# An H3 block with a gated feed-forward: the order of the first loads, the banks of the first transposes, and the first two feed-forward units by halves

## The chip, the cores and the metric

The kernel runs on one core of a Trainium2 chip. The core has TensorE (PE: matrix multiplications and transposes into PSUM), VectorE (DVE), ScalarE (ACT), GpSimd (POOL) and the sync engine (SP, which here issues most DMAs). PSUM has eight banks of 128 partitions x 512 float32; sixteen DMA engines move data between device memory and SBUF. The metric is device time in microseconds of one execution, as a median over runs; lower is better. Before the change it is 215.22 us, the median of 8 runs (214.69 to 217.48).

## The reference

All data is bfloat16, 2048 rows of 512 columns. With `x` = `A_q`, cut to what is computed:

```
xn = layernorm(x)                                   # per row of 512
kv = (4-tap causal shift of k with shift_k) * v     # per column
y  = causal convolution of kv with ssm_k (length 2048, one filter per column) + kv * ssm_D
s  = xn * y
g  = silu( (gelu(xn @ w_gate) * (xn @ w_up)) @ w_down )   # 512 -> 1792 -> 512
out = x + s * g
```

The reference does the convolution with an FFT of length 4096.

## The kernel before

**The convolution.** The kernel does the Fourier transform as matrix multiplications in two stages. Row 16p + t of a tensor lies on partition p of tile t, so there are 16 tiles of 128 x 512. In stage 1 (`stage1`, line 900) each tile t is multiplied by a table F1[t] of cosines and sines (two matmuls of 512 columns); ScalarE copies the result out of PSUM, and a DMA writes it to device memory (ZH for the filter h, ZK for kv), from where stage 2 reads it back in another layout. Stage 2 (`fwd`) multiplies by the table MT. For the filter the result goes to ZS and is read back as HS; for kv it is multiplied with HS on VectorE (line 1015, tile HB), transformed back with MT (`inv`, line 1019), copied by ScalarE (BO), written to ZI and read back as BI; eight last multiplications with G1 (the transposed F1) give y. The filter comes as 512 channels x 2048 taps, so it is first transposed on TensorE: four chunks of 128 channels (tile Hn, loads h0 to h3), each as two halves of 8 transposes (`h_transpose`, line 812, transposes on line 823), copied out as HTr by VectorE or ScalarE. D is added to tap 0 by one VectorE instruction (`h_fold`, line 836). Stage 1 of the filter needs all of HTr and the fold.

**The feed-forward.** The 2048 rows are treated as four quarters q of four tiles. `ln(q)` (line 759) makes mean and variance of each tile on VectorE (bn_stats, line 762; bn_aggr, line 763; variance plus epsilon, line 770), takes the power -0.5 on POOL (line 771) and normalises on VectorE (line 774, tile XN). `xn_transpose(q)` transposes: for q = 0 on TensorE (line 796) in two halves of two tiles, each into a bank and copied to xnT (line 801); for the others by a DMA transpose (line 786). `unit(q, m)` (line 1043) computes 128 of the 1792 hidden columns for a quarter: four matmuls of 512 columns for the gate, four for the up part, Gelu on ScalarE (GE, line 1058), a product on VectorE (HT, line 1061). `down(q)` (line 1064) multiplies HT by w_down, 14 matmuls for each tile, followed by tanh or silu and the products with xn and y.

**Tables.** F1 and MT are made on the chip: iotas on POOL, integer work on VectorE (lines 651 to 669 and 865 to 889), Sin on ScalarE (line 675, 891). Gelu needs another table of ScalarE, so its first use waits until every Sin of F1 is done (`sin_tasks`).

**Order.** The order of instructions on each engine is written by a planner, `Sched.run` (line 313). Each piece of work is a task with an assumed duration, the buffers it needs and a priority (lower goes first). The planner takes the engine that can start earliest, looks at the tasks that could start within SLACK ns of that, and takes the one of lowest priority number; a TensorE task marked `heavy="DVE"` or `"ACT"` has DEFER added when the queue of work for that engine, counted from tasks of priority up to URGENT, is over QUEUE. HEDGE is the delay that it assumes after a DMA for TensorE. The order is then fixed; on the chip each engine works through its list and waits for semaphores. Loads are issued ahead of everything else, in the order of the `load` calls from line 745 on: x of the first quarter as four tiles of 128 KB, h0, h1, the first weight chunk (gate and up), h2, h3, D, the shift taps, and then ORDER (line 25). Most are issued by SP, a few by ACT, whose queue is another ring of the same sixteen DMA engines.

**PSUM.** Pool psF hands out single banks (at most 4 at a time) for units, down tiles and the xn transposes; psC hands out pairs (at most 3) of the same eight banks for the stages and, before the change, for the h transposes. A bank becomes free when the engine that reads it is done.

**Warm-up.** N_WARM matmuls on zeros run before the first data is there.

Of the kernel before, what the change touches and what calls it, by code (L numbers as in the profile page):

```python
# [17 lines left out]
KD = DM // 128  # L18
# [5 lines left out]
N_WARM = 18  # L24
# [235 lines left out]
class Sched:  # L260


    SLACK = 269.06
    SEM = 90.0
    DMA_LAT = 2500.0
    HEDGE = 2000.5
# [4 lines left out]
    QUEUE = {"ACT": 600, "DVE": 4110.2}  # L271
    URGENT = 3.36
    DEFER = 4.48
# [119 lines left out]
def build_kernel(nc, A_q, A_k, A_v, A_shift_k, A_ssm_k, A_ssm_D, B_w_gate, B_w_up, B_w_down, out):  # L393
    with ExitStack() as es0:
# [156 lines left out]
        pC = Pool_("psC", 4, size=2, limit=NC_PAIRS, backing=pF)  # L551
        pGE = Pool_("GE", 3)
# [80 lines left out]
        t_warm = S.add([("PE", 1700.0 + N_WARM * 216.0)], warm_up, r=[bwarm], w=[warm], prio=-9)  # L633
# [70 lines left out]
        FC = [(0, 4), (4, 4), (8, 4), (12, 2)]  # L704
# [7 lines left out]
        def load_x(q):  # L712
            if q:
                load(f"x{q}", X[:, 4 * q:4 * q + 4, :], x_dr[:, 4 * q:4 * q + 4, :], R_X[4 * q:4 * q + 4], bX[q], 524288)
            else:
                for t in range(4):
                    load(f"x{q}_{t}", X[:, t, :], x_dr[:, t, :], R_X[t:t + 1], [bX[0][t]], 131072, ("SP", "ACT")[t % 2])
# [27 lines left out]
        load_x(0)  # L745
        load_h(0, "SP")
        load_h(1, "ACT")
# [11 lines left out]
        def ln(q):  # L759
            pr = (-1, 2, 3.27, 6)[q]  # L760
            for t in range(4 * q, 4 * q + 4):
                op([("DVE", 670.0)], lambda e, h, t=t: h.bn_stats(stats[:, t, :], X[:, t, :]), r=[bX[q][t % 4]], w=[bst[t]], rr=[R_X[t]], ww=[R_st[t]], prio=pr)  # L762
                op([("DVE", 140.0)], lambda e, h, t=t: h.bn_aggr(mv[:, t, 0:2], stats[:, t, :]), r=[bst[t]], w=[bmv[q][t % 4 // 2]], rr=[R_st[t]], ww=[R_mv[t]], prio=pr)
            for h in range(1 if q else 2):
                n = 4 if q else 2
                ts = slice(4 * q + 2 * h, 4 * q + 2 * h + n)
# [3 lines left out]
                op([("DVE", 180.0)], lambda e, hd, ts=ts: hd.tensor_scalar(mv[:, ts, 2:3], mv[:, ts, 1:2], LN_EPS, None, ALU.add), r=bm, w=[be], rr=rm, ww=rm, prio=pr)  # L770
# [10 lines left out]
        def xn_transpose(q):  # L781
            af = gu_tasks[q - 2] if q >= 2 else (mt_last + skb if q else [])
            if q:
# [4 lines left out]
                return  # L788
            for hf in range(2):
                p = B(f"psxn{q}_{hf}", pF)  # L790

                def tr(e, hf=hf, p=p):
                    for j in (2 * hf, 2 * hf + 1):
                        for kd in range(KD):
                            o = bank16(p)[:, 512 * (j % 2) + 128 * kd:512 * (j % 2) + 128 * (kd + 1)]
                            trk.op("PE", lambda h, o=o, kd=kd, j=j: h.transpose(o, XN[:, 4 * q + j, 128 * kd:128 * (kd + 1)], ident[:]),
                                   r=[R_XN[4 * q + j], R_id], w=R_bank(p), accum=True)
                S.add([("PE", 8 * 66.0)], tr, r=[bid] + bXN[4 * q + 2 * hf:4 * q + 2 * hf + 2], w=[p], prio=0, lat=200.0)

                def ev(e, h, hf=hf, p=p):  # L800
                    return copy(e, h, xnT[:, q % 2, 2 * hf:2 * hf + 2, :, :].rearrange("p j k c -> p (j k c)"), bank16(p))
                xnT_tasks.append(op([("DVE", dve(1024, 2)), ("ACT", act(1024))], ev, r=[p], w=[bxnT[q][hf]],
                   rr=lambda p=p: R_bank(p), ww=R_xnT[q % 2][2 * hf:2 * hf + 2], prio=-1, after=af))
# [8 lines left out]
        def h_transpose(k):  # L812
            p = B(f"psh{k}", pC)
            pp = [B(f"psh{k}_{h}") for h in range(2)]

            def tr(hf):
                def f(e):
                    s = psl(p)
                    for j in range(8):
                        t = 8 * hf + j  # L820
                        o = psb(s, 128 * t, 128 * (t + 1))
# [99 lines left out]
        for t in range(NT):  # L921
            stage1("H", t, HTr[:, t, :], R_HTr[t], [bHTr[k][t // 8] for k in range(KD)], ZH, 1.5)
# [289 lines left out]
```

## Time and profile before

| | us |
|---|---|
| median of 8 runs (lowest to highest) | 215.22 (214.69 to 217.48) |
| profiled execution, device time | 214.69 |
| its span, first to last instruction | 212.9 |
| TensorE busy | 204.2 (96%) |
| VectorE busy | 167.9 (79%) |
| ScalarE busy | 119.9 (56%) |
| first transpose of h | 8.20 |
| first matmul of a unit | 11.73 |
| first stage-1 matmul | 20.80 |
| start of the last run of down matmuls | 200.33 |

The profile is one execution, with times from the start of its span. Lines of it name the line of the kernel, the engine, the operation and the tiles (out<-in). Nearly all matmuls are issued in a helper and so have line 590; they are told apart by their tiles: `xnT,Wg` and `xnT,Wu` are the gate and up halves of units, `Wd,HT` down, `HTr,F` and `V,F` stage 1, `BH,MT` and `BK,MT` stage 2, `HB,MT` the way back, `BI,G` the last stage; `ident,Hn` and `ident,XN` are the transposes. Copies are on lines 586 (ScalarE) and 587 (VectorE). PEld is the loading of weights, SPq and ACTq are the queues on which DMAs are issued. A matmul's end is modelled: consecutive ones overlap on paper, and their real spacing is read from a whole group.

### The profile page before, as it was taken

The numbers are of one execution on the slowest core, as the hardware profiler recorded it, in microseconds if no ns is written. First come the engines' busy times: TensorE is split into PE (matmuls) and PEld (weight loads), VectorE is DVE, ScalarE is ACT, GpSimd is POOL, SyncE is SP. The second block draws the span as 40 slices with busy tenths as digits, with TensorE's granted clock in tenths as the row PEclk, the third lists the DMA queues.
The fourth block names the chain that finished last, engine by engine and source line by source line (L and its number), as shares of the span: only waits on it lengthen the run. The fifth ranks groups of instructions, "written<-read, shape, count | busy, mean of one in ns | idle before, by whom it ended". The sixth has DMA issues, their size and how long they took to land.

```text
span 212.9 us, 2881 instructions
## 1 busy us (share of the span) xinstructions
PE 204.2 (96%) x992; PEld 95.5 (45%) x1008; DVE 167.9 (79%) x254; ACT 119.9 (56%) x153; POOL 16.0 (8%) x41
## 2 busy tenths in 40 slices
PE   7797999999999999999999999999999999999993
PEld 2553444444444444444444444444444444444452
DVE  7888788886998989989752877998797783399942
ACT  3588767677777787867847143444534544312221
POOL 8517000001300000000100000000000000000000
PEclk9999999999999999999999999999999999999999
DMA  5999999999799899978899999999998423959312
GB/s 174 376 338 342 375 385 385 413 413 376 181 249 328 262 323 309 319 248 250 284 366 230 307 331 380 341 290 284 284 321 247 173 72 127 313 188 347 116 74 74
DMA packets 49060, 59.57 MB, mean 280 GB/s; under 512 B 13459, under 2 KB 32791, under 8 KB 49046
## 3 DMA queue, kind: packets, MB, share of 16 engines
q1 hardware_dynamic: 41286, 49.16, 72.5%
q10 hardware_dynamic: 7760, 10.23, 13.3%
q8 instruction: 8, 0.13, 0.3%
q14 instruction: 6, 0.05, 0.1%
HBM read 35.78 MB, written 20.97 MB: 267 GB/s over the span
## 4 chain that ended last, share of the span: by engine, by line
PE 65%; DMA 14%; SPq 10%; DVE 7%; issue 1%; ACT 1%; ACTq 0%
PE psall L590 64%; SPq L567 10%; DMA X<-in_A_q_dram 7%; DMA ZI<-BO 3%; DMA Hn<-in_A_ssm_k_dram 3%; DVE HB L1015 2%; DVE stats L762 1%; ACT BO L586 1%; DVE G L1087 1%; PE psall L823 1%; DVE xnT L587 1%; DVE XN L774 1%; DVE F L668 1%; DVE KTM L950 1%; DVE F L669 0%
## 5 line engine op out<-in xcount | busy, mean ns | idle before, releaser
L590 PE MATMUL psall<-xnT,Wu 128*128 128x512 bf16 x224 | 56.7, 379 | 0.0
L1061 DVE TENSOR_TENSOR HT<-psall,GE 128x512 bf16<-128x512 f32 x56 | 38.3, 689 | 22.8 <-PE psall L590 22.7
L590 PE MATMUL psall<-xnT,Wg 128*128 128x512 bf16 x224 | 54.9, 379 | 0.4 <-DVE xnT L587 0.4
L590 PE MATMUL psall<-Wd,HT 128*128 128x512 bf16 (+1 forms) x233 | 52.4, 366 | 0.2
L1058 ACT ACTIVATE GE<-psall 128x512 bf16<-128x512 f32 x56 | 33.0, 600 | 31.6 <-PE psall L590 31.1
L1015 DVE TENSOR_TENSOR HB<-psall,HS 128x1024 bf16<-128x1024 f32 x32 | 36.9, 1218 | 8.0 <-PE psall L590 8.0
L590 PEld LDWEIGHTS psall<-Wd,HT 128*128 128x128 bf16 x238 | 23.3, 98 | 25.3
L590 PEld LDWEIGHTS psall<-xnT,Wg 128*128 128x128 bf16 x224 | 21.8, 98 | 26.5 <-DVE xnT L587 0.6
L590 PEld LDWEIGHTS psall<-xnT,Wu 128*128 128x128 bf16 x224 | 21.8, 98 | 26.0 <-ACT ASH L586 0.3
L586 ACT ACTIVATE BO<-psall 128x1024 bf16<-128x1024 f32 x16 | 16.4, 1024 | 15.0 <-PE psall L590 11.7
L586 ACT ACTIVATE ASH<-psall 128x1024 bf16<-128x1024 f32 x16 | 16.3, 1020 | 3.0 <-PE psall L590 2.6
L590 PE MATMUL psall<-HB,MT 128*128 128x512 bf16 x62 | 16.0, 379 | 0.2
L1085 ACT ACTIVATE G<-psall 128x512 bf16<-128x512 f32 x12 | 7.0, 595 | 15.8 <-PE psall L590 15.8
L952 DVE TENSOR_TENSOR KAC<-KAC,KTM 128x2048 bf16<-128x2048 bf16 x12 | 14.6, 1220 | 0.1
L950 DVE TENSOR_TENSOR KTM<-KK,SKB 128x2048 bf16<-128x2048 bf16 x12 | 14.6, 1218 | 0.0
L762 DVE BATCH_NORM_STATS2 stats<-X 128x6 f32<-128x512 bf16 x16 | 10.4, 673 | 2.1 <-DMA X<-in_A_q_dram 2.1
L771 POOL TENSOR_TENSOR mv<-mv,NHALF 128x4 f32<-128x4 f32 (+1 forms) x5 | 5.3, 1073 | 82.1 <-DVE mv L770 82.0
L980 ACT ACTIVATE AST<-psall 128x1024 bf16<-128x1024 f32 x10 | 10.1, 1023 | 2.4 <-PE psall L590 1.4
L586 ACT ACTIVATE AST<-psall 128x1024 bf16<-128x1024 f32 x10 | 9.9, 1028 | 1.4 <-PE psall L590 1.4
L590 PE MATMUL psall<-HTr,F 128*128 128x512 bf16 x29 | 8.4, 379 | 1.6 <-DVE Q L865 1.5
L590 PEld LDWEIGHTS psall<-HB,MT 128*128 128x128 bf16 x64 | 6.2, 98 | 7.6 <-DVE HB L1015 0.3
L590 PE MATMUL psall<-BH,MT 128*128 128x512 bf16 x30 | 8.4, 379 | 0.1
(73 smaller groups left out, 163.6 us busy)
## 6 DMA issues: line engine op xcount, KB each, us to landing
HS<-ZS SPq DMA_DIRECT2D x16, 512.0 KB, 5.8
ZH<-ASH ACTq DMA_DIRECT2D x16, 256.0 KB, 6.0
BH<-ZH SPq DMA_DIRECT2D x16, 256.0 KB, 4.3
BK<-ZK SPq DMA_DIRECT2D x16, 256.0 KB, 5.3
ZI<-BO ACTq DMA_DIRECT2D x16, 256.0 KB, 4.9
BI<-ZI SPq DMA_DIRECT2D x16, 256.0 KB, 4.4
ZK<-AST SPq DMA_DIRECT2D x10, 256.0 KB, 4.4
ZS<-AST SPq DMA_DIRECT2D x10, 256.0 KB, 4.5
```

The costliest lines, as they stand in the source:

```text
L567: trk.dma(eng, lambda e: e.dma_start(out=out_ap, in_=in_ap), sem, r=r, w=w)
L586: return h.activation(o, i, ACTF.Copy)
L590: return h.matmul(o, lhsT=l, rhs=r, start=st, stop=sp)
L762: op([("DVE", 670.0)], lambda e, h, t=t: h.bn_stats(stats[:, t, :], X[:, t, :]), r=[bX[q][t % 4]], w=[bst[t]], rr=[R_X[t]], ww=[R_st[t]], ...
L771: t_pw = op([("POOL", 800.0)], lambda e, hd, ts=ts, n=n: hd.tensor_tensor(mv[:, ts, 3:4], mv[:, ts, 2:3], NHALF[:, 0:n, :], ALU.pow), r=[b ...
L950: op([("DVE", dur)], lambda e, h, j=j, m=m: h.tensor_tensor(KTM[:, m.slot, :, :], kk(j), sk(j), ALU.mult), r=need + [bSKB, a], w=[m], rr=l ...
L952: op([("DVE", dur)], lambda e, h, m=m: h.tensor_tensor(KAC[:, a.slot, :, :], KAC[:, a.slot, :, :], KTM[:, m.slot, :, :], ALU.add), r=[m], ...
L980: op([("ACT", act(1024))], lambda e, h, p=p, a=a: h.activation(ast["K"][a.slot].rearrange("p c d -> p (c d)"), ps(psl(p)), ACTF.Copy, scal ...
L1015: op([("DVE", dve(1024, 1))], lambda e, h, k=k, pk=pk, qq=qq, hs=hs: h.tensor_tensor(HB[:, qq.slot, :, :].rearrange("p c d -> p (c d)"), p ...
L1058: op([("ACT", act(512))], lambda e, h: h.activation(GE[:, g.slot, :], bank(pg), ACTF.Gelu_apprx_tanh), r=[pg], w=[g], rr=lambda: R_bank(pg ...
L1061: op([("DVE", dve(512, 1))], lambda e, h: h.tensor_tensor(HT[:, q % 2, m, :], bank(pu), GE[:, g.slot, :], ALU.mult), r=[pu, g], w=[bHT[q][m]],
L1085: op([("ACT", act(n))], lambda e, h, g=g, pc=pc: h.activation(g, pc(), ACTF.Tanh, scale=0.5), r=[p], w=[bt], rr=lambda p=p: R_bank(p), ww= ...
```

## The change

- **Loads.** x of the first quarter is issued as tile 0 on ACT and tile 1 on SP, then h0 on SP, tiles 2 and 3 on ACT, and h1 on SP (before: four tiles alternating, h0 on SP, h1 on ACT).
- **Weight chunks.** The hidden columns are loaded in chunks of 2, 4, 4, 4 units instead of 4, 4, 4, 2.
- **First quarter's layernorm.** Tiles 0 and 1 get a more urgent priority than tiles 2 and 3; both xn transposes are listed before both copies.
- **Banks.** The transposes of h and of xn take single banks from a new pool psX (at most 4, of the same eight banks).
- **Halves.** For q = 0, units 0 and 1 are computed in two halves of 256 rows: gate and up of rows 0 to 255, then of rows 256 to 511, each four matmuls of 256 columns into its half of the bank; a half needs only its half of xnT.
- **Warm-up.** 11 matmuls instead of 18.
- **Planner.** SLACK, HEDGE, QUEUE, URGENT, DEFER and several priorities get other values.

```diff
-N_WARM = 18
+N_WARM = 11
...
-    SLACK = 269.06
+    SLACK = 217.65
-    HEDGE = 2000.5
+    HEDGE = 1938.43
-    QUEUE = {"ACT": 600, "DVE": 4110.2}
-    URGENT = 3.36
-    DEFER = 4.48
+    QUEUE = {"ACT": 847.41, "DVE": 7684.62}
+    URGENT = 4.42
+    DEFER = 6.44
...
+        pX = Pool_("psX", 8, limit=4, backing=pF)
...
-        FC = [(0, 4), (4, 4), (8, 4), (12, 2)]
+        FC = [(0, 2), (2, 4), (6, 4), (10, 4)]
...
-        load_x(0)
+        load_x0(0, "ACT")
+        load_x0(1, "SP")
         load_h(0, "SP")
-        load_h(1, "ACT")
+        load_x0(2, "ACT")
+        load_x0(3, "ACT")
+        load_h(1, "SP")
         load_w(0, ("SP", "ACT"))
         load_h(2, "SP")
         load_h(3, "ACT")
...
-            pr = (-1, 2, 3.27, 6)[q]
             for t in range(4 * q, 4 * q + 4):
+                pr = (-1.5, -1)[t // 2] if q == 0 else (-1, 2, 2.93, 6)[q]
...
-                p = B(f"psxn{q}_{hf}", pF)
+            pp = [B(f"psxn{q}_{h}", pX) for h in range(2)]
...
-            p = B(f"psh{k}", pC)
-            pp = [B(f"psh{k}_{h}") for h in range(2)]
+            pp = [B(f"psh{k}_{h}", pX) for h in range(2)]
...
-            stage1("H", t, HTr[:, t, :], R_HTr[t], [bHTr[k][t // 8] for k in range(KD)], ZH, 1.5)
+            stage1("H", t, HTr[:, t, :], R_HTr[t], [bHTr[k][t // 8] for k in range(KD)], ZH, 4.59)
...
-            stage1("K", t, V[:, t, :], R_V[t], [bKV[t // 4]], ZK, 8.39)
+            stage1("K", t, V[:, t, :], R_V[t], [bKV[t // 4]], ZK, 7.22)
...
-            ci = min(m // 4, 3)
+            ci = (m + 2) // 4
...
+            if q == 0 and m < 2:
+                for i in range(2):
+                    for p, W, nm in ((pg, Wg, "g"), (pu, Wu, "u")):
+                        gu_tasks[q].append(S.add([("PE", pe(4, 256))], half(p, W, nm, 2 * i, 2 * i + 2), r=[bW[nm][ci], bxnT[q][i]], w=[p], prio=m + i + 0.95, lat=200.0))
```

Other priorities: the last product of the shift (line 954) 4 to 1.14; stage 2 of the filter 9.33 to 10.49 and of kv 3.66 to 3.71; the products with HS (line 1015) 0.9 to 2.71; the copies BO (line 1026) 0.9 to 2.54; down (line 1080) 9 + q + 2.91 to 9 + q + 1.46; the products of line 1135 6 to 5.73; the copies of xnT -1 to -1.4 and its transposes 0 to -1.

## The prediction

> **What bounds the kernel now.** I first read the shares of the span and the 40 slices, then the order of TensorE's work at the start, then its waits, then busy time by stage, and last the chain that ended the run.
>
> ```profile
> PE 204.2 (96%) x992; PEld 95.5 (45%) x1008; DVE 167.9 (79%) x254; ACT 119.9 (56%) x153; POOL 16.0 (8%) x41
> ...
> PE   7797999999999999999999999999999999999993
> ...
> DMA  5999999999799899978899999999998423959312
> ```
>
> TensorE is busy 96% of the span; only the first four slices and the last are thin. So the time is the point at which TensorE begins to run without gaps, plus a fixed amount of work, plus a tail. The order of its work at the start:
>
> ```profile
> 1.17 5.80 PE L590 MATMUL psall<-AST 128*128 128x512 bf16 x18 [1.17 <-DVE AST L626]
> 8.20 1.70 PE L823 MATMUL psall<-ident,Hn 128*128 128x128 bf16 x24 [1.22 <-DMA Hn<-in_A_ssm_k_dram]
> 9.73 1.06 PE L796 MATMUL psall<-ident,XN 128*128 128x128 bf16 x16
> 10.63 0.66 PE L823 MATMUL psall<-ident,Hn 128*128 128x128 bf16 x8
> 11.73 1.90 PE L590 MATMUL psall<-xnT,Wg 128*128 128x512 bf16 x8 [0.44 <-DVE xnT L587]
> ...
> 17.39 1.89 PE L590 MATMUL psall<-xnT,Wg 128*128 128x512 bf16 x8
> 20.80 1.67 PE L590 MATMUL psall<-HTr,F 128*128 128x512 bf16 x7 [1.51 <-DVE Q L865]
> 22.31 1.89 PE L590 MATMUL psall<-xnT,Wu 128*128 128x512 bf16 x8
> ```
>
> Columns: start, duration, what, and in brackets the wait ahead of it. Real work begins at 8.20, after 1.22 us of waiting for the first chunk of h. A second wait of 1.51 us stands before the first DFT matmuls (HTr,F). By stage:
>
> ```profile
> core 0: us, PE busy (x) PEld busy (x) DVE busy (x) ACT busy (x) POOL busy (x), PEclk, DMA share, GB/s
> 0.00:8.20 8.20, 5.80 (x18) 2.12 (x19) 6.97 (x22) 2.43 (x2) 7.39 (x33) 1.00 0.73 241
> 8.20:20.80 12.60, 10.62 (x105) 7.37 (x106) 10.06 (x27) 11.39 (x13) 4.65 (x6) 1.00 1.06 347
> 20.80:50.50 29.70, 29.59 (x136) 13.40 (x138) 23.23 (x39) 20.90 (x26) 1.04 (x1) 1.00 1.06 396
> 50.50:118.60 68.10, 67.76 (x310) 30.54 (x314) 56.71 (x85) 50.65 (x67) 2.92 (x2) 1.00 0.93 280
> ```
>
> Between 8.20 and 20.80 TensorE idles 2 us; ScalarE (11.39 of 12.60) and the DMA engines are as full as it is. From 20.80 on it idles 0.11 and 0.34 us per stage. The chain of waits shows where a faster start could meet a wall:
>
> ```profile
> 34.78 15.85 DMA X<-in_A_q_dram
> 50.63 0.02 issue
> 50.65 1.29 DVE stats L762 x2
> ```
>
> The third quarter of x lands at 50.63, with the DMA share at 1.06 from 20.80 to 50.50: those loads are bound by bytes, and the change takes none away.
>
> **The measure.** A 512-column matmul costs 0.216 us (46 in 10.10 us of the chain), a transpose 0.066 (24 in 1.70, less the 0.16 by which a modelled end overhangs). By 22.31 TensorE has done 80 transposes (5.28) and 31 matmuls (6.70): 11.98 us of work, so it is 22.31 - 11.98 = 10.33 us "behind". All after that is dense, so what the change takes from this 10.33 it takes from the time, unless later stages give it back.
>
> **The change, part by part.**
>
> *Queues.* SP has five first issues before (x0, x2 of the first rows, h0, gate 0, h2) and five after (x1, h0, h1, gate 0, h2); ACT also five and five. An issue takes 0.43 to 0.51, so ACT's first table load stays at 3.32 and nothing is pushed on either queue: 0.
>
> *First h chunk.* On its queue it now has one 128 KB row tile ahead instead of two. Before, h0 and h1 land at 8.07 and 8.27 with 1.5 MB moved, and both first weight chunks (1 MB more) at 11.0 and 11.35: 0.34 MB/us. If the two queues share by bytes, h0 needs 2 x 640 KB = 1.28 MB: 0.22/0.34 = 0.7 us earlier, 7.4. If they share by packets (the packet records from 4.5 to 5.0 us have 32 of SP's against 36 of ACT's, 119 KB against 54 KB), h0's 128 packets of 4 KB outrun the 1 KB ones of x beside them: 256 + 512 + 128 KB = 0.9 MB, 0.6/0.34 = 1.8 us earlier, 6.3. The first transposes start at 6.3 to 7.4 instead of 8.20.
>
> [...]
>
> *Row tiles 2 and 3.* They land at 5.1 and 5.4 now; by bytes about 6.0, by packets as late as h1, 8.1. Their statistics run at 5.22 and 6.01 and hold VectorE's queue, with the F phases and the normalisations (1.38) behind them. The delay of the second half of xnT is 0.6 to 2.7 us. It is covered: the halved units need only the first half until the first weights land (by packets 8.07 + 0.5/0.34 = 9.6, by bytes 11.0). Without the halves, gate 0 would start that much later. POOL's power steps stand behind its iotas until 7.0 either way.
>
> *First weight chunk of two units.* 512 KB less ahead of h2, h3 and the next chunk: at 0.34 to 0.40 MB/us, 1.3 to 1.5 us. h2 and h3 land at about 12.4 instead of 13.5 and 13.8; the next gate chunk at 16.8 instead of 18.3, its up part at 18.5 instead of 20.0. Units 2 and 3 now need that chunk.
>
> *Halved units.* 32 matmuls of 256 columns at 0.109 (the last tile has 28 of them in the final 9.26 us) for 16 of 512 at 0.216: +0.03. Weight loads of 0.098 still fit under them.
>
> *Single banks.* No transpose waits for a bank now, so the gain is nothing. Ten copies of 0.68 (VectorE) or 1.02 (ScalarE) pass through at most four banks; if all four wait, TensorE waits one copy: 0 to 1.0 lost, beside other waits. I take 0.
>
> *Warm-up.* Seven fewer of 0.216 end it at 5.46 instead of 6.97. Needed, since h0 could land before 6.97. Its cost: the weight loads come 0.43 apart until 4.57 and 0.2 after, so eleven still include three at speed, and the waits of 1.22 and 1.51 left the next work at speed (granted clock 1.00). If the clock were lost once, the eight slow ones show 8 x 0.21 = 1.7 us. Bounds 0 to 1.7; I take 0, since the wait after it, 0.8 to 1.9, is nearest to those two.
>
> [...]
>
> *Sum at the start.* The next weights at 16.8 are when TensorE can be dense. By then 80 transposes and two units (3.49) make 8.77 us of work: 8.0 us behind, a lead of 10.3 - 8.0 = 2.3. The other end: the copies, the Sin tables, Gelu's table load and the fold (1.08) set the pace, as ScalarE's 11.39 of 12.60 says. If gates 2 and 3 still wait until 17.39 for the first Gelu's banks, and half a microsecond more is lost on DFT matmuls that are not ready, it is 9.1 behind: lead 1.2. I take 1.9, nearer the loads, because the copies ahead of the fold get their h2 and h3 1.3 us sooner too.
>
> *Later stages, re-ordered by priorities.* No row shows the new order. What the trace shows are the cushions: xnT of the second quarter is issued at 53.25, lands 4.4 later and is used at 60.52 (cushion 2.9); the first BK lands at 117.0 and is used at 118.62 (1.6); the first BI is issued at 178.48, takes 4.8 and is used at 186.52 (3.2). A lead of 1.9 fits two of them. I take 0.3 lost at BK; bounds: -0.6 (all the remaining idle of the dense part gone) to +3.
>
> Total: 1.9 - 0.3 = 1.6 us. The profiled execution took 214.69 (span 212.9 and 1.79 around it) and would take 213.1; the median of the eight runs, 215.22, stands 0.53 above it, so the median would be 213.6.
>
> **Rivals.**
>
> *Given back at the x loads.* x of the second and third quarters land at 45.36 and 50.65 whatever TensorE does, and VectorE's queue stands 0.58 and 1.54 us for them. With a lead of 1.9 it stands 4.0, and from there to 98 it is about nine tenths busy and cannot catch up. For it: the chain runs through that DMA. Against: from 46 to 60 TensorE has down matmuls, 56 of them, which ask little of VectorE. Left: the BK cushion's worth at most, 0.4: 214.8.
>
> *Slower: the multiplications with H late.* The products of line 1015 go from priority 0.9 to 2.71, behind the HT products (1). Eight pairs of them now come every 7.05 us from 119.04 to 168.37. If each pair lets one more HT product (0.69) go first, the last ZI store and BI are 8 x 0.69 = 5.5 later. It decides from 3.2 on: 2.3 beyond the cushion, plus 0.5 because line 1141's eight products then crowd the tail: 215.2 + 2.8 = 218.0. For it: VectorE is 84% busy there. Against: TensorE could do the last down matmuls first.
>
> *The start does not move.* The fold chain (copies to 19.41, fold to 20.52) is set by ScalarE and VectorE, and units 2 and 3 merely move: lead 0.3, 214.9.
>
> **How the numbers follow.** Lead kept: 0.66, its own range 211.9 to 214.1. Given back at x: 0.10; start unmoved: 0.06; both end within 0.5% (1.08 us, about what a measurement here can tell from none). H products late: 0.18, 216.3 to 219. The dense part might shed its own idle too, hence a low end of 211.6; the high end of 216.4 takes in the two middle cases and the mild end of the slower one. Faster 0.67, same 0.15, slower 0.18.
>
> **What would show it.** First Hn transposes at 6.3 to 7.4; h2's and h3's near 12.4; half-width Wg matmuls before 11; HTr,F before 19; in the dense part the same group of matmuls 1 to 2 us earlier at 40, 100 and 180; the first BI use near 184.6. Wrong if TensorE waits more than 1 us in all after 25, if its weight loads near 8 us stand 0.2 or more apart for want of clock, or if the last HB product ends after 171.

## The result, and the profile after

The changed kernel takes 217.85 us (median of 11 runs, 216.12 to 220.22), beside 215.39 us for the kernel before on the same chip (32 runs). The ratio is 1.0103, 95% interval 1.0073 to 1.0133: slower by 2.2 us. The medians and spreads here and in the table below are of all executions, while every ratio leaves out the few that were in a slow state of the machine. Forecast were 213.6 us and a chance of 0.18 for slower. The profiled execution took 218.37 us, with a span of 216.5 (before: 214.69 and 212.9), so it stands 0.5 above its median and the profile of before 0.5 below its own: a difference of the two profiles (3.7) overstates the change by over 1 us.

The page of the changed kernel: shares of the span, then slices.

```profile
PE 204.2 (94%) x1001; PEld 96.0 (44%) x1017; DVE 171.6 (79%) x254; ACT 120.2 (56%) x153; POOL 16.6 (8%) x41
...
PE   7666999999999999999999899999999999999993
...
DMA  5999999997997369868999999999999324867232
```

TensorE's work is the same 204.2 us. The second to fourth slices read 6, 6, 6 where they read 7, 9, 7: the time went where the change meant to gain it. Lines have moved by one to seven: L591 is now the helper, L824 and L799 are the transposes. TensorE in order of time, from its first real work:

```profile
6.34 1.20 PE L824 MATMUL psall<-ident,Hn 128*128 128x128 bf16 x16 [0.70 <-DMA Hn<-in_A_ssm_k_dram]
8.20 0.90 PE L799 MATMUL psall<-ident,XN 128*128 128x128 bf16 x8 [0.66 <-DVE XN L778]
8.94 1.16 PE L824 MATMUL psall<-ident,Hn 128*128 128x128 bf16 x16
10.31 0.61 PE L591 MATMUL psall<-xnT,Wg 128*128 128x256 bf16 x4 [0.21 <-DVE xnT L588]
12.55 0.61 PE L591 MATMUL psall<-xnT,Wu 128*128 128x256 bf16 x4 [1.63 <-DMA Wu<-in_B_w_up_dram]
13.00 0.60 PE L591 MATMUL psall<-xnT,Wg 128*128 128x256 bf16 x4
13.44 0.61 PE L799 MATMUL psall<-ident,XN 128*128 128x128 bf16 x8
...
20.02 0.38 PE L591 MATMUL psall<-HTr,F 128*128 128x512 bf16 x1 [1.48 <-DVE HTr L588]
21.05 1.84 PE L591 MATMUL psall<-HTr,F 128*128 128x512 bf16 x6 [0.65 <-ACT GE L1065]
22.73 1.89 PE L591 MATMUL psall<-xnT,Wg 128*128 128x512 bf16 x8
```

The first transposes are at 6.34 instead of 8.20 and the first gate matmuls at 10.31 instead of 11.73, as the change intends. Then TensorE stands 1.63 us for the first up weights, with the second xn transposes behind it in its queue, and 1.48 and 0.65 us more before the first DFT matmuls. It is dense from 22.73; before it was from 22.31, with more work done. The chain of waits says why:

```profile
2.13 10.37 DMA Wu<-in_B_w_up_dram
12.51 0.05 issue
12.55 1.05 PE psall L591 x8
13.60 0.46 PE psall L799 x8
14.06 0.02 issue
14.08 0.69 DVE xnT L588
14.77 2.59 DVE F L669
17.37 0.02 issue
17.39 0.44 DVE F L670
17.83 0.02 issue
17.85 1.15 ACT F L676
19.00 0.02 issue
19.02 1.28 ACT L1065
```

Two things stand one behind the other: a load that takes 10.37 us, and one VectorE instruction of 2.59. The second is the first half of an F phase (line 669, a sum of two tables in SBUF), which takes 0.68 or 0.69 us in the three other places where it runs. Its second half is line 670. What ran beside it, in the timeline of all engines:

```profile
14.65 2.16 POOL L927 COPY SKB<-SKR 128x2048 bf16<-128x2048 bf16 x1 [4.20 <-DMA SKR<-in_A_shift_k_dram]
...
14.69 2.67 DVE L669 TENSOR_TENSOR F<-IO,CC 128x1024 int16<-128x1024 int16 x1
```

POOL's copy of the shift taps (SKR to SKB) started 0.04 us ahead of it. The F phase ends 0.55 us after the copy: it lost 1.99 us beside a copy of 2.16. In the kernel before, this copy ran from 18.22 to 20.23, after the F phases; there it held only the small fold (1.08 us at 19.44, and 0.40 in the changed kernel, where nothing of POOL's runs beside it):

```profile
18.22 2.01 POOL L926 COPY SKB<-SKR 128x2048 bf16<-128x2048 bf16 x1
...
19.44 1.08 DVE L836 TENSOR_TENSOR HTr<-HTr,Drow 1x512 bf16<-1x512 bf16 x1
```

**The measure, kept for the runs below.** "Behind" is again the time at which TensorE becomes dense, less the work that it has done by then. One correction: the prediction counted 31 wide matmuls before 22.31. The trace lacks the record of one of them (its eight HTr,F weight loads are there), so it is 32, and the kernel before is 22.31 - 5.28 - 32 x 0.216 = 10.12 behind. The changed kernel has done 80 transposes (5.28), 32 half-width matmuls (3.49) and 8 wide ones (1.73), together 10.50: 22.73 - 10.50 = 12.23. The start loses 2.1 us, about all of the 2.2. A start is read from one execution, though: b1 below has the changed kernel's start unchanged and reads 1.6.

### The profile page after: what moved, and what is told of

It is laid out like the page before. It is cut to its first block, busy times and chain, and to the rows that moved or that the text cites. A ratio compares the mean times of both kernels' runs of the same rounds, so it can differ in the third digit from the quotient of the medians.

```text
span 216.5 us, 2906 instructions
## 1 busy us (share of the span) xinstructions
PE 204.2 (94%) x1001; PEld 96.0 (44%) x1017; DVE 171.6 (79%) x254; ACT 120.2 (56%) x153; POOL 16.6 (8%) x41
## 4 chain that ended last, share of the span: by engine, by line
PE 73%; DMA 15%; ACT 4%; DVE 3%; issue 1%; SPq 1%; ACTq 1%
PE psall L591 73%; DMA ZI<-BO 6%; DMA Wu<-in_B_w_up_dram 5%; DMA ZK<-ASX 3%; DMA BK<-ZK 2%; ACT BO L587 1%; DVE F L669 1%; SPq L568 1%; ACTq L568 1%; ACT GE L1065 1%; ACT L1065 1%; ACT F L676 1%; ACT AST L981 0%; ACT ASX L981 0%; DVE HT L1068 0%
## 5 line engine op out<-in xcount | busy, mean ns | idle before, releaser
L591 PE MATMUL psall<-xnT,Wu 128*128 128x512 bf16 (+1 forms) x232 | 55.6, 372 | 1.6 <-DMA Wu<-in_B_w_up_dram 1.6
L591 PE MATMUL psall<-xnT,Wg 128*128 128x512 bf16 (+1 forms) x232 | 54.1, 372 | 0.2 <-DVE xnT L588 0.2
L591 PE MATMUL psall<-Wd,HT 128*128 128x512 bf16 (+1 forms) x235 | 52.5, 366 | 0.2
L1065 ACT ACTIVATE GE<-psall 128x512 bf16<-128x512 f32 x56 | 32.4, 598 | 27.1 <-PE psall L591 27.1
L1016 DVE TENSOR_TENSOR HB<-psall,HS 128x1024 bf16<-128x1024 f32 x32 | 37.5, 1217 | 5.6 <-PE psall L591 5.6
L591 PEld LDWEIGHTS psall<-xnT,Wu 128*128 128x128 bf16 x232 | 22.5, 98 | 27.6 <-DMA Wu<-in_B_w_up_dram 1.9
L591 PEld LDWEIGHTS psall<-Wd,HT 128*128 128x128 bf16 x238 | 23.2, 98 | 25.4
L591 PEld LDWEIGHTS psall<-xnT,Wg 128*128 128x128 bf16 x232 | 22.6, 98 | 26.0 <-DVE xnT L588 0.3
L591 PE MATMUL psall<-HB,MT 128*128 128x512 bf16 x60 | 15.9, 379 | 0.6 <-ACT BO L587 0.4
L953 DVE TENSOR_TENSOR KAC<-KAC,KTM 128x2048 bf16<-128x2048 bf16 x12 | 14.6, 1220 | 0.2
L951 DVE TENSOR_TENSOR KTM<-KK,SKB 128x2048 bf16<-128x2048 bf16 x12 | 14.6, 1218 | 0.0
L1094 DVE SCALAR_TENSOR_TENSOR G<-G,psall 128x512 bf16<-128x512 bf16 x12 | 8.1, 684 | 6.0 <-ACT G L1092 5.8
L591 PE MATMUL psall<-HTr,F 128*128 128x512 bf16 x29 | 8.6, 380 | 2.3 <-DVE HTr L588 1.5
L1100 ACT ACTIVATE G<-psall 128x512 bf16<-128x512 f32 (+1 forms) x5 | 2.6, 512 | 13.2 <-PE psall L591 13.2
```

The source lines that it names most:

```text
L591: return h.matmul(o, lhsT=l, rhs=r, start=st, stop=sp)
L951: op([("DVE", dur)], lambda e, h, j=j, m=m: h.tensor_tensor(KTM[:, m.slot, :, :], kk(j), sk(j), ALU.mult), r=need + [bSKB, a], w=[m], rr=l ...
L953: op([("DVE", dur)], lambda e, h, m=m: h.tensor_tensor(KAC[:, a.slot, :, :], KAC[:, a.slot, :, :], KTM[:, m.slot, :, :], ALU.add), r=[m], ...
L1016: op([("DVE", dve(1024, 1))], lambda e, h, k=k, pk=pk, qq=qq, hs=hs: h.tensor_tensor(HB[:, qq.slot, :, :].rearrange("p c d -> p (c d)"), p ...
L1065: op([("ACT", act(512))], lambda e, h: h.activation(GE[:, g.slot, :], bank(pg), ACTF.Gelu_apprx_tanh), r=[pg], w=[g], rr=lambda: R_bank(pg ...
L1094: op([("DVE", dve(512, 1))], lambda e, h, g=g, pc=pc: h.scalar_tensor_tensor(out=g, in0=g, scalar=1.0, in1=pc(), op0=ALU.add, op1=ALU.mult ...
```

## The experiments

Each ratio is to the kernel before, run on the same chip beside it. The starts are worked out as above, from one profile each. The profiles read a mean granted TensorE clock of 1.00, but 0.984 in a2, 0.985 in b1 and 0.992 in a4 and d3.

| run | edit | median us | ratio [95%] | dense at | start against before |
|---|---|---|---|---|---|
| changed kernel | | 217.85 | 1.0103 [1.0073, 1.0133] | 22.73 | +2.1 |
| a1 | taps' copy held | 216.73 | 1.0031 [0.9999, 1.0062] | 20.72 | +0.1 |
| e2 | first up weights and h3 on SP | 216.50 | 1.0019 [0.9987, 1.0051] | 21.36 | +0.7 |
| d1 | both | 215.43 | 0.9977 [0.9950, 1.0005] | 19.89 | -0.7 |
| a2 | first ten loads as before | 218.94 | 1.0128 [1.0067, 1.0190] | 23.28 | +2.7 |
| a3 | a1 and a2 | 216.93 | 1.0017 [0.9982, 1.0051] | 19.88 | -0.7 |
| a4 | 18 warm-ups | 218.75 | 1.0109 [1.0056, 1.0162] | 23.00 | +2.4 |
| d2 | a3, 18 warm-ups | 215.97 | 1.0014 [0.9985, 1.0044] | 21.53 | +0.9 |
| d3 | before, new order of loads | 216.42 | 1.0030 [1.0001, 1.0059] | 23.61 | +1.3 |
| d4 | before, 11 warm-ups | 216.68 | 1.0029 [0.9993, 1.0065] | 23.91 | +1.6 |
| c1 | before, taps' copy held | 215.55 | 1.0004 [0.9973, 1.0035] | 21.44 | -0.9 |
| c2 | before, new planner values | 219.81 | 1.0169 [1.0122, 1.0215] | 21.38 | -0.1 |
| c3 | changed, old planner values | 217.54 | 1.0092 [1.0060, 1.0125] | 21.95 | +1.3 |
| e1 | d1, old planner values | 216.72 | 1.0054 [1.0023, 1.0085] | 19.66 | -1.0 |
| b1 | BK loads issued early | 226.04 | 1.0483 [1.0442, 1.0524] | 22.20 | +1.6 |

**a1: POOL's copy after VectorE's last F phase.** The theory: the copy is the cause. The rival: the late weights are. The copy is put behind the last F phase in the order and waits for VectorE there.

```diff
+        def skb_hold(f=skb[0].emit):
+            D = trk.engs["DVE"]
+            with nc.body(trk.engs["POOL"]["body"]):
+                trk._do_waits("POOL", {D["sem"].name: (D["seq"], trk.evid, D["sem"])})
+            f("POOL")
+        skb[0].emit = lambda e: skb_hold()
...
+        i, j = order.index(skb[0]), order.index(ph_tasks[3])
+        if i < j:
+            order.insert(j, order.pop(i))
```

> The changed kernel with one more wait: POOL's copy of the shift taps (line 927) starts only when VectorE has done the last F phase. The order on every engine is kept. Theory P (the copy holds up VectorE): in the changed kernel the last F phase took 2.67 us instead of 0.68, ending 0.6 us after the copy beside it. Without that the last Sin ends 2.0 us earlier, Gelu's first use comes at 18.3 instead of 20.3, TensorE is dense from 20.8 instead of 22.7: the time falls by 1.5 to 2.0 us, to about 216. Rival Q (the last chunk of h, landing at 15.5 instead of 13.8, sets the start): the last F phase is short again, but the fold and the first DFT matmuls stay where they are (20.0) and the time falls by less than 0.5 us.

Measured: 216.73 us, ratio 1.0031. The timeline of a1:

```profile
14.54 0.68 DVE L669 TENSOR_TENSOR F<-IO,CC 128x1024 int16<-128x1024 int16 x1
...
16.35 2.06 POOL L928 COPY SKB<-SKR 128x2048 bf16<-128x2048 bf16 x1 [5.74 <-DVE HTr L588]
...
20.72 1.89 PE L591 MATMUL psall<-xnT,Wg 128*128 128x512 bf16 x8
```

The F phase is back at 0.68, and TensorE is dense 2.0 us earlier, at 20.72. 0.72% of the time returns, 1.55 us (the two intervals leave about 0.9 either side): the copy is a cause. It now meets the fold instead, which takes 1.16 us and not 0.40, but TensorE's next wait is for Gelu and not for the fold. But the start only equals that of before; its chain of waits still begins with the first up weights (10.22 us from issue to landing).

**e2 and d1: the first up weights and h3 on SP's queue.** In the changed kernel these two go by ACT's queue, and h3 lands 12.9 us after its issue. Both runs move them, in the same order, to SP's; d1 also holds the copy.

```diff
+        FIRST_LOADS = [('x0_0', 'ACT'), ('x0_1', 'SP'), ('h0', 'SP'), ('x0_2', 'ACT'), ('x0_3', 'ACT'), ('h1', 'SP'), ('wg0', 'SP'), ('wu0', 'SP'), ('h2', 'SP'), ('h3', 'SP')]
...
+            ring = dict(FIRST_LOADS).get(name, ring)
```

> The changed kernel with POOL's copy of the taps held until VectorE's last F phase is done (as in a1), and with the first up weight chunk and h3 on SP's queue instead of ACT's, in the same order. Theory that ACT's queue is starved beside SP's larger packets: up weights land before 11.5 instead of 12.5 and h3 before 14 instead of 15.5, TensorE's stop of 1.3 to 1.6 for Wu falls below 0.5. Whether that is worth time is the question: if the chain F phase, Sin, Gelu, GE, HT sets the dense start (20.72 in a1), the start gains at most 0.3 and the time stays at 216.4 to 217.0; if the late landings set it, dense from 19.5 or earlier and 215.0 to 215.8.

> The changed kernel with only the first up weight chunk and h3 on SP's queue; POOL's copy stays where it is. d1 was 0.9977 with both causes undone, a1 1.0031 with the copy held alone, the changed kernel 1.0103. Theory that the two add up: the landings alone give back 0.5 to 1.2 us, 216.6 to 217.3, ratio 1.003 to 1.008. Rival, that the copy beside the last F phase sets the dense start whatever lands when: VectorE's last F phase still takes 2 or more and the time is as the changed kernel's, 217.4 to 218.2, ratio 1.008 to 1.013. A third: VectorE's chain runs earlier and the copy, which waits for nothing of VectorE's, meets other VectorE work or none, so that the cost moves or goes.

Measured: e2 1.0019, d1 0.9977. The DMA issues of the first 20 us, with KB each and median us from issue to landing, in the changed kernel:

```profile
Hn<-in_A_ssm_k_dram ACTq DMA_DIRECT2D x1, 512.0 KB, 12.9
...
Wu<-in_B_w_up_dram ACTq DMA_DIRECT2D x1, 256.0 KB, 10.4
```

and in e2:

```profile
Hn<-in_A_ssm_k_dram SPq DMA_DIRECT2D x4, 512.0 KB, 6.6
...
Wu<-in_B_w_up_dram SPq DMA_DIRECT2D x1, 256.0 KB, 7.1
```

On SP's queue the same 256 KB of up weights land 7.1 us after issue instead of 10.4, and no h chunk takes over 7.8. TensorE no longer waits for Wu. VectorE gets to its last F phase at 13.49 instead of 14.69. That is a cause by itself: alone it gives back 0.84%, 1.8 us (again with about 0.9 either side), more than the 0.5 to 1.2 expected. Which of the two loads does it was not tried. But the copy then meets the other half of the phase, a TENSOR_SCALAR with one input, and holds it as long. The timeline of e2:

```profile
13.49 0.68 DVE L674 TENSOR_TENSOR F<-IO,CC 128x1024 int16<-128x1024 int16 x1
...
14.01 2.15 POOL L932 COPY SKB<-SKR 128x2048 bf16<-128x2048 bf16 x1 [3.61 <-DMA SKR<-in_A_shift_k_dram]
...
14.20 2.24 DVE L675 TENSOR_SCALAR F<-F 128x1024 int16<-128x1024 int16 x1
...
21.36 1.89 PE L596 MATMUL psall<-xnT,Wg 128*128 128x512 bf16 x8
```

With both undone, d1's TensorE in order:

```profile
16.64 0.59 PE L596 MATMUL psall<-HTr,F 128*128 128x512 bf16 x2
18.21 1.84 PE L596 MATMUL psall<-HTr,F 128*128 128x512 bf16 x6 [0.98 <-ACT GE L1078]
19.89 1.89 PE L596 MATMUL psall<-xnT,Wg 128*128 128x512 bf16 x8
```

The start is 0.7 us ahead of the kernel before, and d1 is the fastest of all: 2.7 us below the changed kernel (1.0103 - 0.9977), and 0.5 us below the kernel before, which its interval does not quite separate from none. The expectation for d1 had two theories. The time fits the second (215.0 to 215.8): the late landings set what a1 left. Its mark for the start, 19.5 or earlier, was missed by 0.4, and what now bounds the start is the table chain of the first: on ScalarE the last Sin at 15.02, the load of Gelu's table (1.28 us at 16.18), and the first Gelu at 17.47 (16.29 in the kernel before).

**a2 and a3: the old order of loads.** The rival that the order of the loads alone is to blame: the first ten loads go out in the old order and on the old queues (the same edit with another list), in a3 with the copy held as well.

> The changed kernel with the ten first loads in the order and on the queues of the kernel before (x tiles alternating, h0 and gate 0 and h2 on SP, h1 and up 0 and h3 on ACT); the chunks of two units, the halves, the banks and every engine's order stay. Rival Q: h3 lands before 14 instead of at 15.5 and the first up chunk before 11 instead of at 12.5, and the time falls by 1 to 1.7 us. Theory P: h0 lands later (8 instead of 6.2) without loss, the last F phase still stands beside the copy of the taps or, if that copy moves with its load, next to it; the time changes by less than 0.7 us.

> The changed kernel with both: POOL's copy of the taps held back behind the last F phase, and the first ten loads in the order and on the queues of the kernel before. Theory P (the copy is what moved the start; the loads matter little): as with the copy alone, dense from 20.3 to 20.8, ratio to the kernel before 1.003, within 0.4%. Rival Q (with the copy out of the way the late up chunk, a wait of 1.3 us, and h3 set the start): the loads of before bring another 0.7 to 1.3 us, ratio 0.997 to 1.000.

a2 is no better than the changed kernel (1.0128). TensorE doesn't wait for up weights there, but the first h chunk lands late again, and the copy holds VectorE (2.23 us for the TENSOR_SCALAR). Its DFT matmuls come at 20.78 and are slow: six took 2.71 us, where the same six take 1.84 in the changed kernel. Its first 16 transposes are slow too, 1.90 us instead of 1.20, after TensorE stood 2.82 us for the h chunk; the granted clock reads 0.72 from 6 to 12 us and 0.65 from 20 to 23. So a2 doesn't tell what its landings alone are worth. a3 holds the copy as well and starts 0.7 ahead, as d1 does, with 1.0017, between its two expectations. Its profile is the fastest of its 12 executions, 214.76 us at a granted clock of 1.00; 9 of the 12 read 0.984 to 0.992. So the old order is no cure by itself. With the copy held it brings the start as far as the new queue of the two loads does.

**d3: the new order of loads in the kernel before.**

> The kernel before, its plan kept, with only the order and the queues of its first ten loads changed to those of the changed kernel (x tile 0 on ACT, 1 on SP, then h0 on SP, x tiles 2 and 3 on ACT). h0 lands near 6.2, which 18 warm-ups until 8.2 hide; x tiles 2 and 3 near 8.1, up weights near 12.5, h3 near 15.5. Theory that these landings are a cost by themselves: TensorE waits 0.5 to 1.2 for Wu and h3 and the time is 215.9 to 216.6. Rival, that the old plan covers them (its up matmuls begin at 14.2): within 0.5 of the kernel before, 214.9 to 215.9.

1.0030: here it costs 0.65 us, within the expected range though the interval all but reaches none, and by another way than stated. TensorE waits neither for Wu nor for h3, but for the later row tiles:

```profile
6.59 1.88 PE L828 MATMUL psall<-ident,Hn 128*128 128x128 bf16 x24
10.54 1.68 PE L801 MATMUL psall<-ident,XN 128*128 128x128 bf16 x16 [2.08 <-DVE XN L779]
12.01 1.06 PE L828 MATMUL psall<-ident,Hn 128*128 128x128 bf16 x8
13.00 2.63 PE L595 MATMUL psall<-xnT,Wg 128*128 128x512 bf16 x8
```

Without the halves, TensorE needs row tiles 2 and 3 before its first unit, and stands 2.08 us. This is the cost that the halved units cover in the changed kernel. After the stop TensorE is also slow for some microseconds: 16 transposes take 1.68 us instead of 1.06 and 8 gate matmuls 2.63 instead of 1.90.

**a4, d4 and d2: the warm-up.**

```diff
-N_WARM = 11
+N_WARM = 18
```

(a4, on the changed kernel; d4 does the reverse on the kernel before, and d2 the same as a4 on a3. The planner's assumed duration stays, so the order doesn't change.)

> The changed kernel with 18 warm-up matmuls instead of 11, in the same order. If eleven are too few in some executions, runs of the changed kernel with a mean granted clock of 0.992 (0.8% of 216 us at half speed is 1.7 us lost) go away, and the spread of the times narrows; the median falls by 0.3 to 1 us. If eleven suffice: no change, or up to 0.6 us slower, since the first transposes (6.34) then wait for the warm-up's end at 6.97.

> The kernel before, its plan kept, with 11 warm-up matmuls instead of 18. TensorE then stands idle from about 6.3 until the first h chunk's transposes at 8.2, which the trace shows waiting for that chunk. Theory that the count of warm-ups keeps the clock: some executions at 0.990 to 0.992, up to 1.7 longer, and a median of 215.5 to 217. Theory that the count does not matter: clock 0.997 or more, 214.9 to 215.9.

> a3 (taps' copy held, first ten loads in the old order and queues) with 18 warm-up matmuls instead of 11; the first h chunk lands at 7.8 there, so the longer warm-up delays nothing. a3's executions were split, some at a granted clock of 1.0 with 214.8 to 214.9 and some at 0.990 to 0.992 with 215.0 to 217.3. Theory that the thin first 8 us with 11 warm-ups lose the clock: all executions at 0.997 or more, median 214.7 to 215.2, ratio below 1.000. Theory that the idle stretch around 18 to 21 loses it: still split, median 216 to 217, ratio 1.001 to 1.005.

Seven more warm-ups give the changed kernel nothing (1.0109 against 1.0103), and executions with a lower clock don't go away: two of six read 0.990 and 0.992, beside 4 of 12 of the changed kernel at 0.992. In d2 they do go away, as the first theory had it: all 12 read 0.997 or more, where 9 of a3's read less. But its ratio is a3's (1.0014 against 1.0017), and not the one below 1.000 that this theory gave. In d2's profile the same first h chunk took 7.5 us to land instead of a3's 5.9, which fits its start of +0.9. In a4's profile, one of the two at the lower clock, six DFT matmuls are as slow as in a2, after waits of 1.40 and 0.65 us; after 1.48 and 0.65 the changed kernel's took 1.84:

```profile
20.49 2.71 PE L591 MATMUL psall<-HTr,F 128*128 128x512 bf16 x6 [0.65 <-ACT GE L1065]
```

So the number of warm-ups at the start doesn't decide it there. Seven fewer in the kernel before cost the start 1.6 us. The order of TensorE in d4:

```profile
8.07 2.75 PE L823 MATMUL psall<-ident,Hn 128*128 128x128 bf16 x24 [2.03 <-DVE F L669]
10.62 1.91 PE L796 MATMUL psall<-ident,XN 128*128 128x128 bf16 x16
12.33 1.06 PE L823 MATMUL psall<-ident,Hn 128*128 128x128 bf16 x8
```

The 24 transposes take 2.75 us instead of 1.70, the 16 of xn 1.91 instead of 1.06 and the 8 after them 1.06 instead of 0.66: 2.3 us lost by slow matmuls after an idle stretch of 2.03 us. In the end d4 is at 1.0029, and the interval reaches 1.000: most of it is won back later; where was not looked into. The mean granted clock is a poorer witness than these durations. It read 0.982 to 0.992 in 7 of d4's 12 executions and in none of the 35 of the kernel before beside it; but among d4's executions those at full clock were not the faster ones, and its profiled one, with the slow transposes, has 1.00, in the stretches of the start too.

**c1: the copy held back in the kernel before**, until the fold is done.

> The kernel before with POOL's copy of the taps held back until VectorE has added D to HTr (the fold, line 836). There the fold took 1.08 us beside the copy; in the changed kernel, with the copy over, 0.40. Theory P: the fold takes 0.40, the first DFT matmul comes at 20.1 instead of 20.8, and the time falls by 0.3 to 0.7 us. If the wait moves to the Gelu banks or the shift products wait for the copy (2 us later), 0 to 0.5 us is lost instead.

1.0004: no difference. The fold takes 0.41 us and TensorE is dense 0.9 us earlier in its profile. But the copy, now at 19.71, meets the next VectorE instructions on the tables: the pair on line 882 (MT from MT and Q) takes 2.21 us instead of 0.42. The products behind it come late, and TensorE waits 0.50 us for one of them at 24.26. So holding the copy there only moved the collision.

**c2, c3, e1: the planner's values and the priorities of the later stages.** The rival that the change loses its time in the new order of the later stages: in c2 the kernel before gets the new values, in c3 the changed kernel gets the old ones, and in e1 so does d1.

```diff
-    SLACK = 269.06
+    SLACK = 217.65
...
-    QUEUE = {"ACT": 600, "DVE": 4110.2}
+    QUEUE = {"ACT": 847.41, "DVE": 7684.62}
...
-    URGENT = 3.36
-    DEFER = 4.48
+    URGENT = 4.42
+    DEFER = 6.44
```

> The kernel before with the changed kernel's planner constants and priorities of later stages only (SLACK, HEDGE, QUEUE, URGENT, DEFER and the priorities from the third quarter's layernorm to the products of line 1135); loads, chunks, halves, banks, warm-up and the first quarter's priorities as before. Theory R (the constants cost something of their own after 23 us): slower by 1 us or more, waits of TensorE between 100 and 150 as in the changed kernel. Rival S (the loss is the start's alone): within 0.6 us of the kernel before.

> The mirror image: the changed kernel with the planner constants and later priorities of the kernel before. All of the start's changes stay. Theory R: 1 to 1.5 us faster than the changed kernel, about 216.5, since only the start's loss (1.9 us at 22.7) is left. Rival S: as slow as the changed kernel, 217.5 to 218. If the two sets belong together (each set fits its own start), both this and its mirror image are slower than their bases by 1 us or more.

> The changed kernel with the planner's constants and the later stages' priorities of the kernel before (as in c3), POOL's copy of the taps held until VectorE's last F phase is done, and the first up weight chunk and h3 on SP's queue (both as in d1). In d1's profile TensorE starts 0.9 ahead of the kernel before at 25 and still ends later, after waits of 0.9 for BK at 119, 1.2 and 0.9 for BO at 136 and 144. Theory that the new constants cost the later stages: with the old ones those waits go to 1.0 in all, and the time is 213.8 to 214.9, ratio 0.990 to 0.996. Rival, that the plan re-forms around any start and loses it elsewhere (as c3, which with the old constants was no faster than the changed kernel): 215.0 to 216.3, ratio 0.996 to 1.003.

c2 is 1.69% slower than the kernel before, with a start no later than that one's; its waits are scattered over the later stages. TensorE's weight loads in c2:

```profile
55.40 0.55 PEld L590 LDWEIGHTS psall<-Wd,HT 128*128 128x128 bf16 x4 [1.28 <-ACT AST L586]
...
124.31 0.13 PEld L590 LDWEIGHTS psall<-BH,MT 128*128 128x128 bf16 x2 [1.45 <-ACT GE L1058]
```

That would make the values the culprit, if the reverse held. It doesn't: putting the old ones back changes the changed kernel by 0.1% (c3), less than can be told, and makes d1 slower, 1.0054 instead of 0.9977 (e1, whose weight loads wait 1.08 us at 24.73 for a product of VectorE). So the new values are not why the changed kernel is slow: the set made for the other kernel costs 1.7% in c2 and 0.8% in e1, and gives nothing in c3. Which single value does it in c2 was not tried, and its profile is the fastest of its six executions (217.27 us).

**b1: the first six BK loads issued right behind the last ZK store.** In the changed kernel TensorE waits 0.79 us at 122.33 for BK; the idea was to issue these loads earlier on SP.

```diff
+        for t in bk_loads[:6]:
+            order.remove(t)
+        at = 1 + max(order.index(t) for t in zk_tasks)
+        order[at:at] = bk_loads[:6]
```

> The changed kernel with the first six BK loads issued on SP right after the last ZK store, instead of behind the DMA transpose of xnT and stores that wait for ScalarE. The rest of the order is kept. Theory R (part of the loss is made at 116 to 123, by SP's queue): the first stage-2 matmuls of kv no longer wait (0.79 us at 122.33), and the time falls by 0.8 us. Rival S (the whole loss is made before 23): nothing beyond 0.3 us, the wait moves to the next thing.

226.04 us, a clear miss. In b1 SP has nothing to show between 106.2 and 113.28: it waits for stores of ZK to land, and everything behind it waits too, among it a load of BH that TensorE needs sooner:

```profile
112.86 1.89 PE L591 MATMUL psall<-xnT,Wg 128*128 128x512 bf16 x8
122.70 1.01 PE L591 MATMUL psall<-BH,MT 128*128 128x512 bf16 x2 [7.96 <-DMA BH<-ZH]
```

## Why the prediction was wrong

**The step that failed is "Sum at the start".** It had TensorE dense at 16.8, 8.0 behind, a lead of 1.9 (ends 1.2 and 2.3). The measured start is 22.73, 12.23 behind: 2.1 us lost. The list of parts behind the sum lacked one term and had another wrong.

- *The lacking term.* POOL was named once ("POOL's power steps stand behind its iotas until 7.0 either way"), and its copy of the taps was costed nowhere. The page of before showed it: 2.01 us at 18.22, beside a fold of 1.08 us for a row of 512 elements. The same smaller first chunk that was to bring h2 sooner brings the taps sooner too (14.6 instead of 15.5). More than that, the planner moved the copy up in POOL's order: before, it stood behind POOL's work on PHI and MSK until 18.22, well after the taps had landed; now it starts as soon as they land, and meets VectorE's last F phase. a1 puts it at 1.55 us of the time.
- *The wrong term.* "First h chunk" gave two ends, by bytes and by packets, and the packets were right: 6.34 against 6.3. But "First weight chunk" was then reckoned as if all loads shared alike. What h0 gained, ACT's queue lost. From 2 to 6.3 us SP's queue moved 0.94 MB and ACT's 0.29: the up half of the first chunk was expected near 9.6 and landed at 12.5, h3 near 12.4 and landed at 15.5. Only what goes by SP came as expected (gate half 9.7, h2 12.0). Halving the chunk didn't help there either: 512 KB of up weights took 9.2 us to land from ACT's queue before, 256 KB take 10.4 now. The rows of the smaller chunk are 512 bytes and not 1 KB, so it has as many packets as the larger one: from 8 to 9 us ACT's queue moves 261 packets in 0.13 MB, where before, from 9 to 10, it moved 167 in 0.17. e2 puts this cause at 1.8 us when undone alone; together with the copy it is 2.7, not 3.35. Intervals of this width don't tell whether the two overlap.

The start is then the lead of 0.7 that d1 and a3 show. That is below the lower end of the step, 1.2, so the gain would have been mis-sized even without the two causes: d1's TensorE still waits 0.98 us and more before the DFT matmuls, for Gelu and the bank that it frees. The term that was too large here is the pace of the tables: the prediction took 1.9, "nearer the loads", and not the 1.2 of its other end. The rival "the start does not move", with a lead of 0.3, was nearer.

The sum had no term for what POOL's copy does to VectorE. An F phase instruction that started after the copy ended 0.28 to 0.55 us behind it: 2.67 us instead of 0.68 for the sum of two tables, 2.24 instead of 0.43 for the TENSOR_SCALAR. Copies out of PSUM beside the same POOL copy lost nothing (0.67 to 0.69 each). In a2 an F phase started first, at 14.59, and kept its 0.68; the copy, at 14.75, took 2.50 us instead of 2.0 to 2.2. No run shows what the two engines contend for.

Point by point for the rest:

- *Queues*, 0: wrong in the rows, without cost. The issues of h2 and h3 took 1.41 and 1.45 us instead of 0.51 and 0.64, so ACT's first table load came at 4.10 and not at 3.32, but nothing on the path waited for that. What was missed lies in the sharing. The prediction's counts of packets from 4.5 to 5.0 us are also slightly off: the profile of before has 34 of SP's and 30 of ACT's there, 0.13 MB against 0.07, which bears the same reading.
- *Row tiles 2 and 3*: right for TensorE. They came as late as the packets made them (the last at 8.15) and the halves covered it; d3 shows the 2.08 us that it costs without them. VectorE's queue is another matter: in d1 the chain that ends at the dense start begins with a row tile (5.41 us from issue to landing) and runs through VectorE's statistics, F phases and copies, then Sin and Gelu. In a3, with the row tiles early and h0 late, the chain begins with h0 and the start is the same.
- *Halved units* (+0.03) and *single banks* (0): no wait for a bank of transposes shows, and the matmuls take what was reckoned.
- *Warm-up*, 0 of 0 to 1.7: right for this kernel, as a4 shows, and the first transposes run at speed (16 in 1.20 us). The 1.7 was a fair upper end: with the first h chunk as late as before, eleven warm-ups cost the start 1.6 us (d4). The wait after them is 0.70 us here; 1.60 did no harm in a3, 2.03 did in d4.
- *Later stages*, 0.3 lost: by the medians, 2.2 less 2.1 leaves 0.1; by the two profiles, where the last TensorE work ends at 212.71 instead of 209.06, 1.5. So the size can't be told, and the place is mixed: 0.79 us at BK, as named, and 0.37 at 146.44 for BO. The runs with a good start give back some of it too: a3 is 1.1 us slower than its start says, d1 0.2, though d1's profile waits 1.2 us for BO and 0.5 for BK after 22 us, where the kernel before has no such wait. d3 and d4 win 0.7 and 1.0 back.
- *Rival "H products late"*, 218.0: near in time and wrong in kind. It was to come from the priority 2.71 of the products with HS. d1 keeps that priority and by the medians ends no later than the kernel before. The first BI matmul was indeed 2.6 later (189.1 against 186.5), but behind a start 2.1 late.
- *"Given back at the x loads"*: not seen. VectorE no longer waits for x of the second and third quarters in the changed kernel.
- *The marks*: Hn at 6.3 to 7.4 and half-width Wg before 11 came true. The transposes of h2 and h3 near 12.4 did not: h2 landed at 12.0, but they ran at 13.88 and 15.61. Nor did HTr,F before 19 (20.02) or the first BI near 184.6 (189.1); TensorE's waits after 25 come to over 1 us. The mark "last HB product ends after 171" was badly set, as the kernel before ends it at 173.0 itself.

What stays open: whether d1 is faster than the kernel before at all, what its later waits cost, and which of the new planner values costs the kernel before its 1.7%.

## What to carry to other kernels

When a change moves loads forward, list every instruction that a load releases, on the idle engines as well: a 2 us copy on an 8% busy POOL held the start up by as much, because it ran beside the one VectorE instruction on the path. Before such a copy is moved, look at what it will meet next: in c1 it met another instruction and nothing was gained. Here a load moved ahead took its time from the other queue (the up half landed at 12.5, where 9.6 was expected): cost what the other queue holds by the packet sizes on both, and try the load that is needed first on the queue with the larger packets, where 256 KB landed 7.1 us after issue instead of 10.4. Planner values that were set for one order say nothing about another: try them on the kernel that they were made for.

## What the hardware showed that was not expected

- A POOL copy of 128 x 2048 bfloat16 (2.0 to 2.2 us) held VectorE instructions on SBUF data that started after it until it had ended: 2.67 instead of 0.68 us for the sum of two tables, 2.24 instead of 0.43 for the TENSOR_SCALAR, 1.08 to 1.16 instead of 0.40 for the one-row fold, 2.21 instead of 0.42 for the pair in c1. Not every one: in c2 a TENSOR_SCALAR of 128 x 1 (Q, at 18.30) took 0.14 beside the copy (17.80 to 19.84), and 0.13 where no copy runs.
- Two queues on the same sixteen engines shared by packets and not by bytes. In the changed kernel, from 2 to 6.3 us, SP's moved 0.94 MB in 336 packets and ACT's 0.29 MB in 317; from 8 to 12 us 0.97 MB in 477 and 0.58 MB in 465. With 4 KB packets of h on SP's beside 1 KB packets of x on ACT's, 256 KB on ACT's queue took 10.4 us to land, and 7.1 on SP's.
- TensorE ran slowly after some idle stretches and not after others. Behind eleven warm-ups, waits of 0.70 (changed kernel), 1.50 (d1) and 1.60 us (a3) left the first 16 transposes at 1.18 to 1.20 us; 2.82 made them 1.90 (a2), and 2.03 made 24 take 2.75 instead of 1.70 (d4). Behind eighteen, 2.16 us did no harm in d2, and a stop of 2.08 did in d3. Of four like pairs of waits ahead of the DFT matmuls, 2.05 to 2.33 us together, two were followed by slow matmuls (a2, a4) and two not (changed kernel, e2). What decides it was not tested. The clock column of a profile doesn't always show it: from 20 to 23 us it reads 0.65 in a2 and 0.59 in a4, but 1.00 all along d4's slow transposes.
- Six loads moved ahead on SP's queue cost b1 8.2 us against the changed kernel, by the load that then stood behind their wait.
